# A gated-attention and MLP kernel on one core: the second step's angles copied into the carry tile, five full products for a pair's phases, and a new order table

## The chip, the core and the metric

The kernel runs on one core of a Trainium2 chip. The metric is the device time of one execution in microseconds (us), the median of several runs. One execution was also taken with the hardware profiler; its instructions are shown here by engine: PE (matmul), PEld (the loads of the matmul's weights), DVE, ACT, POOL, and SP, which issues most of the DMAs. PE, DVE, ACT, POOL and SP each run their own instructions strictly in the order in which the program has them, and wait for each other by semaphores.

## The reference

Inputs are q, k, v and a complex gate a (a_re, a_im), each 4 batches x 8 heads x 768 steps x 48. Per batch and head a complex state is multiplied by the gate at each step, k times v is added, and q reads the real part:

```python
mag = np.sqrt(a_re * a_re + a_im * a_im)
scale = np.minimum(mag, 0.999) / (mag + 1e-06)
for t in range(S):
    new_re = ar * S_re - ai * S_im          # ar, ai: the scaled gate at t
    new_im = ar * S_im + ai * S_re
    S_re, S_im = (new_re + kv, new_im)      # kv = outer(k[t], v[t])
    y[:, :, t] = einsum('bhd,bhde->bhe', q[:, :, t], S_re)
```

The heads are then put side by side to x (4 x 768 x 384), and out = x + relu(layernorm(x) * g_ln @ w_ch1) @ w_ch2, with a hidden width of 1536.

## The kernel before

**Tiling.** The steps are cut into chunks of 128; two chunks make a pair. There are 3 pairs per batch and 12 in all, P = 0 to 11; chunk n = 2P + c. Pair 0 is made in two halves of the heads, the others in one piece. The recurrence becomes matmuls: with the running sums of the log magnitudes and of the angles of the gate, k and q are scaled by exp and turned by sine and cosine, and a masked product of the two gives the chunk's part; a state G is carried from chunk to chunk.

**Stages of a pair**, by the names in the order table: `are`, `aim`, `k`, `q`, `vf` are loads. `ln`, `iv`, `r`, `r2`, `u`, `l`, `lc` make the log magnitudes; `dec` sums them on PE, and `e` and `en` are their exponentials. `th` is the angle by arctangent (ACT). `ph` sums the angles on PE into phases; `sin`, `abs`, `cos` (for pairs 0 to 2 a PE step `qt` in place of `abs`) turn them into sine and cosine. `ke`, `qe` scale k and q, `ks`, `qs` multiply by cosine (suffix .0) and sine (.1). `ksT`, `qsT` are the transposes of those, for some chunks on PE (`kT`, `qT`, then a copy), for others by a DMA that SP issues (L617). `am` is the product of chunk n (L635), `atm` its mask on DVE, `gm` and `G` the state, `y` and `x` the chunk's output, `bn` and `rstd` the layer norm, `xtr` and `xT` the transpose of x, `mm1` (L740) and `relu` the first layer, `mm2` (L772), `oa`, `ot`, `st` the second and the store. `wl`, `wp`, `wc` load and prepare the weights once. `warm` is a filler: a product on constants whose result nobody reads.

**Phases.** A pair's tile of angles `th` has on partition p the two steps 2p and 2p+1 (j = 0 and 1). The phase of step t in chunk c is a sum over all earlier steps, so chunk 0 needs partitions 0 to 63 alone, and chunk 1 needs all 128. The sum over the pairs before comes from the tile `car`, of which `pick` selects a row; `car` holds values on partitions 96 to 127 that the pair before has written, and a constant elsewhere. For a pair after the first this makes six products of 384 columns (L498 to L507): three on half of the partitions (64 rows), then three on 128 (or, in a batch's first pair, 96 for the last):

```python
(0, u_th[lo, 0, 0], th[0][lo], True, False),
(1, (pick_f if first else pick)[hi], car[hi], True, False),
(0, u_th[lo, 0, 1], th[1][lo], False, False),
(1, u_th[:, 1, 0], th[0], False, False),
(1, u_th[:, 1, 1], th[1], False, True),
(0, pick[rows], car[rows], False, True)):
```

**Order.** The table `PLAN` names every step once with its engine (P, A, V, G for POOL, S for SP) and, for PSUM users, a bank. The program is emitted in the table's order, so the table sets the order on each engine's queue, and which engine does a step. `@x` behind a step makes it wait for step x as well. Tiles come from small rings (two `car`, two `th`, three `ks`, and so on). Fillers stand in the table where its maker left room on PE.

Of the kernel before, what the change touches and what calls it, by code (L numbers as in the profile page):

```python
# [49 lines left out]
warm.54:P0 warm.55:P0 warm.56:P0 warm.57:P0 dec.1.0:P2 ident:G pad.ks.1:G@pickf en.1.0:A2 q.1.0:S r.2.0:V warm.58:P0  # L50
warm.59:P0 warm.60:P0 warm.61:P0 warm.62:P0 warm.63:P0 warm.64:P0 warm.65:P0 warm.66:P0 warm.67:P0 warm.68:P0
warm.69:P0 warm.70:P0 warm.71:P0 warm.72:P0 warm.73:P0 warm.74:P0 warm.75:P0 dps.0:P5 mask:G are.3.0:S r2.2.0:V
e.1.0:A2 dps.1:P7 ke.0.1.0:V u.2.0:A tab.trig.1:A pad.qs.1:G th.0.1:A vf.0.1:S ke.0.0.0:V th.0.0:A th.1.0:A warm.76:P0
warm.77:P0 warm.78:P0 warm.79:P0 warm.80:P0 warm.81:P0 warm.82:P0 warm.83:P0 warm.84:P0 warm.85:P0 warm.86:P0
# [5 lines left out]
q.2.0:S warm.102:P0 warm.103:P0 warm.104:P0 warm.105:P0 warm.106:P0 warm.107:P0 wp.0:P1 en.2.0:A4 ks.0.0.1:V  # L60
qe.1.0.0:G@qs.0.0.0 car.1.0:V6 wc.0.0:V1 kT.0:P2 e.2.0:A4 wc.0.2:V1 qT.0:P3 vf.1.0:S qt.1.0:P6 vf.1.1:S qsT.0:V3
qT.1:P5 ln.3.0:A qs.1.0.1:G warm.108:P0 warm.109:P0 warm.110:P0 warm.111:P0 kT.1:P3 are.4.0:S ksT.0:A2 q.2.1:S
wc.0.1:V1 qsT.1:V5 iv.3.0:A wl.2:G ksT.1:V3 warm.112:P1 am.0:P0 k.2.1:S aim.4.0:S k.2.0:S warm.113:P2 ph.2.0:P4
am.1:P2 tab.trig.3:A atm.0:V0 atm.1:V2 cos.1.0:A6 v.0:G ke.1.0.1:G warm.114:P0 warm.115:P0 gm.0:P7 y.0:P1 sin.2.0:A4
warm.116:P0 warm.117:P0 qt.2.0:P4 G.0:A7 x.0:A1 qs.1.0.0:V gm.1:P7 y.1:P2 cos.2.0:A4 r.3.0:G xtr.0:P6 x.1:A2
ks.1.0.0:V warm.118:P0 qT.3:P1 pad.qs.2:G qT.2:P4 v.1:G th.3.0:A ks.1.0.1:V xT.0:V6 r2.3.0:G@xT.0 xtr.1:P3 kT.3:P0
qsT.3:V1 wp.2:P6 wl.3:G@xT.0 ksT.3:V0 q.3.1:S qsT.2:A4 tab.log.4:A kT.2:P2 qe.2.0.1:G qe.2.0.0:G am.3:P4 xT.1:V3
G.1:V7 mm1.0.0.1:P0 mm1.0.0.0:P0 one:G@ke.0.1.0 ksT.2:A2 gm.2:P7 relu.0.0:A0 wc.2.0:V6 atm.3:V4 wc.2.2:V6 G.2:A7
mm1.0.1.1:P2 ln.4.0:A am.2:P4 mm1.0.1.0:P2 wc.2.1:V6 y.3:P6 relu.0.1:A2 ph.3.0:P0 iv.4.0:A atm.2:V4 x.3:V6 gm.3:P7
y.2:P6 qs.2.0.1:V x.2:A6 xtr.3:P2 mm1.0.2.1:P4 wl.4:G@atm.2 xtr.2:P3 car.3.0:V0 q.3.0:S r.4.0:G are.6.0:S mm1.0.2.0:P4  # L70
bn.1:V xT.3:V2 xT.2:V3 abs.3.0:A0 mm1.1.1.0:P2 u.3.0:A bn.3:V G.3:V7 relu.0.2:V4 mm1.1.1.1:P2 tab.trig.5:A relu.1.1:A2
mm1.1.2.1:P6 sin.3.0:A0 k.3.0:S bn.2:V mm1.1.2.0:P6 k.3.1:S mm1.1.0.0:P3 cos.3.0:A qs.2.0.0:V are.5.0:S mm1.1.0.1:P3
wl.5:G@qs.2.0.1 l.3.0:V th.4.0:A r2.4.0:V lc.3.0:V qT.5:P2 qT.4:P1 ke.2.0.1:G relu.1.2:V6 mm2.0.0:P5 mm2.0.1:P5
relu.1.0:A3 ke.2.0.0:G ks.2.0.0:G@r2.4.0 tab.log.6:A mm2.1.0:P3 u.4.0:A bn.0:V dec.3.0:P6 rstd.0:A mm2.1.1:P3 qsT.4:V1
e.3.0:A6 mm2.1.2:P3 vf.2.1:S vf.2.0:S qsT.5:V2 l.4.0:V k.4.0:S lc.4.0:V en.3.0:A6 qe.3.0.0:V aim.5.0:S qe.3.0.1:V
vf.3.1:S vf.3.0:S mm2.0.2:P5 ks.2.0.1:G kT.5:P0 dec.4.0:P6 ot.0:V5 oa.1:A3 aim.6.0:S are.7.0:S mm2.2.0:P3 rstd.1:A
dps.3:P5 ksT.5:A0 qs.3.0.0:V qs.3.0.1:V kT.4:P1 decc.3:V5 mm2.2.1:P3 qT.6:P0 ke.3.0.0:V ksT.4:V1 e.4.0:A6 ln.6.0:A
dps.4:P4 qT.7:P2 k.4.1:S mm2.3.0:P1 mm2.2.2:P3 ke.3.0.1:G@ke.3.0.0 ks.3.0.1:V en.4.0:A6 ks.3.0.0:V decc.4:V4 iv.6.0:A
qsT.7:V2 q.4.1:S ln.5.0:A ot.2:V3 v.2:G@ot.2 am.4:P4 ph.4.0:P6 ke.4.0.0:G atm.4:V4 kT.6:P2 qsT.6:A0 gm.4:P0
ot.1:G@atm.4 am.5:P3 ksT.6:V2 mm2.3.1:P1 q.4.0:S kT.7:P5 G.4:V0 iv.5.0:A atm.5:V3 car.4.0:A6 mm2.3.2:P1 r.5.0:G  # L80
tab.trig.7:A abs.4.0:A6 y.4:P2 vf.4.1:S v.3:G sin.4.0:A6 x.4:A2 th.5.0:A ksT.7:V5 st.0:S vf.4.0:S r.6.0:G st.1:S
ot.3:V1 y.5:P0 am.6:P6 x.5:V0 xtr.4:P4 are.8.0:S am.7:P2 xtr.5:P1 q.5.1:S gm.6:P0 xT.4:V4 r2.5.0:G atm.6:V6 cos.4.0:A
ph.5.0:P4 atm.7:V2 xT.5:A1 qe.4.0.1:G@xT.4 G.6:A0 mm1.2.1.0:P6 y.6:P1 q.5.0:S x.6:V1 mm1.2.1.1:P6 mm1.2.2.1:P2
sin.5.0:A4 relu.2.1:V6 abs.5.0:A4 gm.7:P0 G.7:V0 y.7:P4 mm1.2.2.0:P2 aim.7.0:S r2.6.0:A x.7:V4 bn.5:V ke.4.0.1:G
th.6.0:A cos.5.0:A mm1.2.0.0:P0 xtr.7:P5 xT.7:V5 qe.4.0.0:G@atm.6 xtr.6:P4 mm1.2.0.1:P0 xT.6:V4 relu.2.2:A2
tab.log.8:A k.5.0:S qs.4.0.1:V u.5.0:A relu.2.0:V0 k.5.1:S qs.4.0.0:V ks.4.0.0:V mm1.3.1.0:P2 mm1.3.1.1:P2
mm1.3.0.1:P4 l.5.0:V mm1.3.0.0:P4 relu.3.1:A2 ks.4.0.1:V mm2.4.0:P1 ksT.8:S lc.5.0:V u.6.0:A relu.3.0:A4 l.6.0:V
ln.7.0:A mm2.4.1:P1 mm2.5.0:P6 qsT.9:S vf.5.1:S aim.8.0:S v.4:G dec.5.0:P4 mm1.3.2.0:P2 kT.9:P7 iv.7.0:A lc.6.0:V
mm2.5.1:P6 gm.8:P0 e.5.0:A4 ln.8.0:A bn.4:V en.5.0:A4 mm1.3.2.1:P2 bn.7:V mm2.4.2:P1 G.8:V0 bn.6:V relu.3.2:A2 st.2:S
dec.6.0:P4 ksT.9:V7 r.7.0:G qT.8:P2 qsT.8:V2 rstd.2:A k.7.1:S mm2.6.0:P7 k.6.0:S gm.9:P0 qe.5.0.1:G@G.8 en.6.0:A4  # L90
ke.5.0.0:G iv.8.0:A e.6.0:A4 mm2.6.1:P7 r2.7.0:A am.8:P2 k.6.1:S qe.5.0.0:G mm2.5.2:P6 are.9.0:S q.7.0:S G.9:V0
ke.5.0.1:G@qsT.8 ot.4:V1 rstd.3:A q.6.1:S u.7.0:A am.9:P4 vf.5.0:S atm.8:V2 tab.trig.9:A atm.9:V4 ot.5:V6 ph.6.0:P0
th.7.0:A car.6.0:V0 y.8:P2 mm2.6.2:P7 mm2.7.0:P4 y.9:P3 sin.6.0:A0 x.9:A3 mm2.7.1:P4 x.8:V2 qs.5.0.0:G r.8.0:G
abs.6.0:A0 ks.5.0.0:V xtr.8:P5 mm2.7.2:P4 qs.5.0.1:V xT.8:V5 th.8.0:A oa.7:A4 st.3:S ke.6.0.0:G@qs.5.0.1 qT.11:P3
ot.6:V7 xtr.9:P2 bn.9:V xT.9:V2 cos.6.0:A ph.7.0:P0 car.7.0:A0 dps.6:P2 st.4:S abs.7.0:A0 r2.8.0:A ks.5.0.1:V
mm1.4.1.1:P4 mm1.4.1.0:P4 mm1.4.0.1:P6 bn.8:V ke.6.0.1:G qsT.11:V3 kT.11:P3 ksT.10:S q.6.0:S ks.6.0.1:V sin.7.0:A0
relu.4.1:A4 mm1.4.0.0:P6 mm1.4.2.1:P0 mm1.4.2.0:P0 l.7.0:V ksT.11:V3 relu.4.0:A6 tab.log.10:A v.5:V lc.7.0:V
dec.7.0:P4 decc.6:V2 qT.10:P3 ks.6.0.0:V qe.6.0.1:G@ks.6.0.0 aim.9.0:S e.7.0:A4 ln.9.0:A vf.6.0:S gm.10:P6 en.7.0:A4
# [113 lines left out]
def kernel(  # L212
# [123 lines left out]
    def c_pickf():  # L336
        nc.vector.memset(pick_f, 0.0)
        nc.vector.memset(pick_f[ds(HALF, 1)], 1.0)
# [503 lines left out]
```

## Time and profile before

| | |
|---|---|
| three runs | 189.17, 189.30, 191.72 us; median 189.3 |
| the profiled execution's own time | 188.27 us |
| its span (first to last instruction) | 186.6 us, so 1.67 us lie around it |
| PE busy | 176.6 us (95%), 2040 matmuls |
| DVE, ACT, POOL busy | 158.3 (85%), 156.2 (84%), 96.3 (52%) |
| granted clock of PE | 1.0 in every slice |
| moved by DMA | 37.23 MB |

A matmul's own length in the trace is a latency: matmuls overlap, and the next starts before the last has ended. What a matmul costs PE is the time from its start to the next one's start. In the chain of waits a piece is the time until the next piece begins, so pieces there can be added.

### The profile page before, as it was taken

Reading aid. Unit: us, or ns where it says so; the run is one execution under the profiler, and the core shown is the slowest. Engines: PE = TensorE matmul, PEld = TensorE weight load, DVE = VectorE, ACT = ScalarE, POOL = GpSimd, SP = SyncE. Lnnn points to the kernel's source line nnn. Section 1 sums busy time; section 2 is a strip of 40 time slices with the busy share of each in tenths; the row PEclk is TensorE's granted clock in tenths of the full one; section 3 lists DMA queues with packets and bytes.
Section 4 is the critical chain, followed back from the end, with each engine's and each line's share of the span. In section 5 each row is a group of like instructions: output and inputs, shape, how many; then the busy total and the mean of one; then the engine's idle time right before and its main releaser. Section 6 shows DMA issues by size and latency. Waiting matters only on the chain.

```text
span 186.6 us, 5141 instructions
## 1 busy us (share of the span) xinstructions
PE 176.6 (95%) x2040; PEld 136.9 (73%) x2040; DVE 158.3 (85%) x292; ACT 156.2 (84%) x223; POOL 96.3 (52%) x117
## 2 busy tenths in 40 slices
PE   5899999999999999999999999999999899798992
PEld 4678677888676897767877787878868577685772
DVE  0699999999989999889999899988999777576463
ACT  5789999999999999999999999989999878243220
POOL 8137387686614990596058660750613408521650
PEclk9999999999999999999999999999999999999999
DMA  5999999899899998999999999999989999996423
GB/s 141 291 227 186 244 224 220 174 204 233 149 216 251 209 275 185 201 223 210 179 233 228 164 203 282 184 231 181 204 186 195 193 196 182 233 117 168 142 93 127
DMA packets 131799, 37.23 MB, mean 200 GB/s; under 512 B 125888, under 2 KB 131776, under 8 KB 131776
## 3 DMA queue, kind: packets, MB, share of 16 engines
q1 hardware_dynamic: 128272, 33.76, 87.5%
q0 software_dynamic: 2784, 2.36, 8.6%
q10 hardware_dynamic: 720, 0.79, 1.2%
q8 instruction: 16, 0.26, 0.6%
q14 instruction: 7, 0.06, 0.1%
HBM read 28.31 MB, written 4.72 MB: 177 GB/s over the span
## 4 chain that ended last, share of the span: by engine, by line
PE 71%; DMA 13%; DVE 8%; SPq 3%; ACT 2%; issue 1%; POOL 0%; DVEq 0%
PE banks L772 23%; PE banks L740 20%; PE banks L612 5%; PE banks L506 5%; PE banks L635 5%; DMA qsT<-qs 5%; DMA w1b<-in_moe_w_ch_dram 4%; PE banks L481 3%; DMA aim<-in_a_im_dram 3%; PE banks L685 3%; DMA ksT<-ks 2%; DVE w1b L392 2%; PE banks L688 2%; PE banks L706 2%; PE banks L663 2%; SPq L449 1%
## 5 line engine op out<-in xcount | busy, mean ns | idle before, releaser
L772 PE MATMUL banks<-w2b,h 128*128 128x384 bf16 (+1 forms) x300 | 54.6, 319 | 0.0
L740 PE MATMUL banks<-xT,w1b 128*128 128x256 bf16 x432 | 51.3, 272 | 0.1
L740 PEld LDWEIGHTS <-w1b 128*128 128x128 bf16 x432 | 41.2, 98 | 6.4 <-DVE xT L290 0.8
L772 PEld LDWEIGHTS <-h 128*128 128x128 bf16 x300 | 26.8, 97 | 12.4
L293 DVE TENSOR_TENSOR atm<-banks,mask 128x1024 bf16<-128x1024 f32 x24 | 28.9, 1219 | 5.0 <-PE banks L635 4.8
L757 ACT ACTIVATE h<-banks 128x1024 bf16<-128x1024 f32 (+1 forms) x25 | 24.9, 1006 | 8.8 <-PE banks L740 8.5
L293 POOL TENSOR_TENSOR ke<-k,en 128x384 bf16<-128x384 f32 x17 | 16.7, 990 | 16.7 <-ACT en L485 4.6
L810 ACT ACT_TABLE_LOAD x18 | 23.1, 1283 | 1.1 <-PEq L826 0.8
L805 PE MATMUL banks<-u_e 128*128 128x256 f16 x119 | 17.5, 299 | 2.5 <-POOL u_e L322 2.2
L759 DVE TENSOR_SCALAR h<-banks 128x1024 bf16<-128x1024 f32 (+1 forms) x12 | 14.0, 1176 | 4.2 <-PE banks L740 4.1
L635 PE MATMUL banks<-qsT,ksT 128*128 128x128 bf16 x192 | 14.6, 219 | 2.7 <-DMA qsT<-qs 1.7
L293 POOL TENSOR_TENSOR qe<-q,e 128x384 bf16<-128x384 f32 x13 | 11.9, 920 | 10.1 <-DVE ks L293 5.4
L805 PEld LDWEIGHTS <-u_e 128*128 128x128 f16 x119 | 12.5, 107 | 4.9 <-POOL u_e L322 1.9
L635 PEld LDWEIGHTS <-ksT 128*128 128x128 bf16 x192 | 12.2, 97 | 4.8 <-issue 2.3
L785 POOL TENSOR_TENSOR ot<-ot,x 128x384 f32<-128x384 f32 x11 | 11.0, 1003 | 6.2 <-DVE x L290 4.3
L293 POOL TENSOR_TENSOR r<-aim,are 128x768 f16<-128x768 f32 x6 | 10.9, 1815 | 6.0 <-ACT are L454 6.0
L288 ACT CAST x<-banks 128x384 bf16<-128x384 f32 x16 | 7.7, 484 | 7.1 <-PE banks L688 6.2
L698 DVE BATCH_NORM_STATS2 stats<-x 128x6 f32<-128x384 bf16 x24 | 13.2, 550 | 0.3 <-ACT x L288 0.3
L293 POOL TENSOR_TENSOR qs<-qe,trig 128x768 bf16<-128x768 bf16 x6 | 10.4, 1727 | 6.0 <-DVE qe L293 2.9
L418 POOL TENSOR_SCALAR v<-vf 128x768 bf16<-128x768 f32 x8 | 6.7, 839 | 12.8 <-DMA vf<-in_v_dram 10.1
L470 DVE SCALAR_TENSOR_TENSOR l<-r,w 128x768 f16<-128x768 f16 (+1 forms) x13 | 12.4, 954 | 0.7 <-ACT r L466 0.6
L685 PE MATMUL banks<-v,atm 128*128 128x48 bf16 x192 | 11.9, 183 | 0.0
(100 smaller groups left out, 385.9 us busy)
## 6 DMA issues: line engine op xcount, KB each, us to landing
k<-in_k_dram SPq DMA_DIRECT2D x24, 192.0 KB, 4.3
q<-in_q_dram SPq DMA_DIRECT2D x24, 192.0 KB, 4.5
vf<-in_v_dram SPq DMA_DIRECT2D x24, 192.0 KB, 4.1
are<-in_a_re_dram SPq DMA_DIRECT2D x11, 384.0 KB, 5.3
aim<-in_a_im_dram SPq DMA_DIRECT2D x11, 384.0 KB, 4.4
out_dram<-ot SPq DMA_DIRECT2D x20, 192.0 KB, 3.3
w1b<-in_moe_w_ch_dram POOLq DMA_DIRECT2D x3, 384.0 KB, 6.7
w2b<-in_moe_w_ch_dram POOLq DMA_DIRECT2D x3, 384.0 KB, 7.8
```

What stands on the lines that cost most here:

```text
L293: {"DVE": nc.vector, "POOL": nc.gpsimd}[eng(name)].tensor_tensor(**kw)
L470: nc.vector.scalar_tensor_tensor(out=S_("l"), in0=S_("r2"), scalar=0.5, in1=S_("w"), op0=ALU.mult, op1=ALU.add)
L635: nc.tensor.matmul(ps[:, h], lhsT=T("ksT", n)[:, h], rhs=T("qsT", n)[:, h], start=True, stop=True)
L685: nc.tensor.matmul(ps[:, h], lhsT=T("atm", n)[:, h], rhs=T("v", P)[:, c, h], start=True, stop=nfirst)
L698: nc.vector.bn_stats(out=T("stats", n), in_=T("x", n))
L740: nc.tensor.matmul(ps[:, jj], lhsT=w1b[:, dc, ts(gi * JG + jj, C)], rhs=T("xT", P)[:, dc].rearrange("p c t -> p (c t)"), start=(dc == 0), ...
L757: act(out=dst, in_=src, func=AF.Relu)
L759: nc.vector.tensor_scalar(out=dst, in0=src, scalar1=0.0, scalar2=None, op0=ALU.max)
L772: nc.tensor.matmul(bank(own)[:, 0:w], lhsT=T("h", P)[:, j, ts(c, C)], rhs=w2b[:, j, es], start=(j == 0), stop=(j == NJ - 1))
L785: nc.gpsimd.tensor_tensor(out=T("ot", n)[:, es], in0=T("ot", n)[:, es], in1=T("x", n)[:, es], op=ALU.add)
L805: g.add(f"warm.{i}", lambda i=i: nc.tensor.matmul(bank(f"warm.{i}")[:, 0:256], lhsT=u_e[:, 0, 0], rhs=u_e[:, 1].rearrange("p j t -> p (j t ...
L810: g.add(f"tab.{nm}.{i}", lambda tab=tab: nc.scalar.preload_act_table_set(tab))
```

## The change

Two new constant matrices, `u_car` and `u_car_f`, have the sum matrix of chunk 0's second step in rows 0 to 63 and the rows of `pick` (or `pick_f`) in rows 64 to 127. A new step `tc.P` copies the second step's angles of partitions 0 to 63 into partitions 0 to 63 of `car`, where `pick` has zeros. One full product with `u_car` then does what two products did, and the list for a pair after the first has five products, all on 128 rows.

```diff
+    u_car = pool.tile([C, C], FP16, name="u_car")
+    u_car_f = pool.tile([C, C], FP16, name="u_car_f")
...
+    def c_ucar():
+        for t, p in ((u_car, pick), (u_car_f, pick_f)):
+            nc.vector.tensor_copy(out=t[HALF:C], in_=p[HALF:C])
+            nc.vector.tensor_copy(out=t[0:HALF], in_=u_th[0:HALF, 0, 1])
...
+    g.add("ucar", c_ucar, needs=["uth", "pick", "pickf"])
...
+            if NS == 1:
+                def f_tc(X=X, fs=fs, step=step):
+                    dst, src = heads(T("car", P)[0:HALF, fs]), step(T("th", P), 1)[0:HALF]
+                    if eng(f"tc.{X}") == "POOL":
+                        nc.gpsimd.tensor_scalar(out=dst, in0=src, scalar1=1.0, scalar2=0.0,
+                                                op0=ALU.mult, op1=ALU.add)
+                    else:
+                        put(f"tc.{X}", dst, src)
+                add(f"tc.{X}", f_tc, needs=[f"th.{X}", f"car0.{P % RINGS['car']}"],
+                    uses=[("th", P), ("car", P)])
...
-                    lo, hi, th = slice(0, HALF), slice(HALF, C), [step(T("th", P), j) for j in range(R)]
+                    th = [step(T("th", P), j) for j in range(R)]
...
-                            (0, u_th[lo, 0, 0], th[0][lo], True, False),
-                            (1, (pick_f if first else pick)[hi], car[hi], True, False),
-                            (0, u_th[lo, 0, 1], th[1][lo], False, False),
-                            (1, u_th[:, 1, 0], th[0], False, False),
-                            (1, u_th[:, 1, 1], th[1], False, True),
-                            (0, pick[rows], car[rows], False, True)):
+                            (0, u_th[:, 0, 0], th[0], True, False),
+                            (1, u_th[:, 1, 0], th[0], True, False),
+                            (1, u_th[:, 1, 1], th[1], False, False),
+                            (0, u_car_f if first else u_car, car, False, True),
+                            (1, pick_f if first else pick, car, False, True)):
...
             add(f"ph.{X}", f_ph, needs=[f"th.{X}", "uth", "pick", "pickf", f"car0.{P % RINGS['car']}"]
+                + ([f"tc.{X}", "ucar"] if NS == 1 else [])
```

The table `PLAN` is replaced as a whole. It has 1158 steps where it had 1143: eleven `tc` (8 on POOL, 2 on DVE, that of pair 1 on ACT), `ucar` on DVE, and 122 fillers for 119. Among the other steps some change engine: `G.0` goes from ACT to DVE, `G.10` and `G.12` the other way; `abs.10` and `car.10` go from DVE to ACT; `relu.11.0` and `relu.11.1` go from DVE to ACT; `ks.9.0.0` goes from DVE to POOL. Two tokens of the new table: `tc.5.0:G@ksT.7` and `ks.9.0.0:G@xT.17`. The order moves on every engine; three places are shown.

**PE, the phases of pair 4.** `th_92` holds the angles of pair 4, `car_167` its carry. Before:

```order
L506 LDWEIGHTS u_th
L506 MATMUL banks<-th_92,u_th 128x384
L506 LDWEIGHTS pick
L506 MATMUL banks<-car_167,pick 128x384
L506 LDWEIGHTS u_th
L506 MATMUL banks<-th_92,u_th 128x384
L506 LDWEIGHTS u_th
L506 MATMUL banks<-th_92,u_th 128x384
L506 LDWEIGHTS u_th
L506 MATMUL banks<-th_92,u_th 128x384
L506 LDWEIGHTS pick
L506 MATMUL banks<-car_167,pick 128x384
```

and after:

```order
L526 LDWEIGHTS u_th
L526 MATMUL banks<-th_92,u_th 128x384
L526 LDWEIGHTS u_th
L526 MATMUL banks<-th_92,u_th 128x384
L526 LDWEIGHTS u_th
L526 MATMUL banks<-th_92,u_th 128x384
L526 LDWEIGHTS u_car
L526 MATMUL banks<-car_167,u_car 128x384
L526 LDWEIGHTS pick
L526 MATMUL banks<-car_167,pick 128x384
```

The first three of the six were on 64 rows each; all five of the new ones are on 128, and the carry's two stand last.

**DVE and POOL, where k of pair 9 is turned** (`ks_110` is its tile, written once by cosine and once by sine; `car_168` is the carry that pair 10 leaves). DVE before:

```order
L293 TENSOR_TENSOR ks_110<-ke_107,trig_101 128x16x48
L698 BN_STATS stats_142<-x_138 128x6
L699 BN_AGGR mv_149<-stats_142 128x2
L290 COPY xT_156<-banks 128x3x128
L527 TENSOR_SCALAR car_168<-banks 32x384
L293 TENSOR_TENSOR ks_110<-ke_107,trig_101 128x16x48
L551 TENSOR_REDUCE sh_104<-banks 128x768
```

DVE after:

```order
L295 TENSOR_TENSOR qs_113<-qe_109,trig_101 128x16x48 x2
L295 TENSOR_TENSOR ke_107<-k_73,en_100 128x384
L295 TENSOR_TENSOR ks_110<-ke_107,trig_101 128x16x48
L292 COPY xT_156<-banks 128x3x128
L292 COPY dec_94<-banks 48x8 x2
L809 SCALAR_TENSOR_TENSOR ot_162<-banks,rstd_153,x_137 128x384
```

and POOL after:

```order
L295 TENSOR_TENSOR qe_109<-q_70,e_98 128x384
L806 TENSOR_TENSOR ot_165<-ot_165,x_135 128x384
L295 TENSOR_TENSOR ks_110<-ke_107,trig_101 128x16x48
L428 TENSOR_SCALAR v_79<-vf_77 128x768
L295 TENSOR_TENSOR ke_106<-k_74,en_99 128x384
L506 TENSOR_SCALAR car_168<-th_93 64x384
```

The second of the two multiplications stood on DVE behind the carry of pair 10; it now stands on POOL, and the carry has gone to ACT. The last POOL row is one of the new copies, that of pair 11.

**ACT, the last part of the program** (`h_161` is the hidden layer of pair 11; the DMA rows are stores that ACT issues itself). Before:

```order
L778 ACTIVATE ot_162<-banks,rstd_151 128x384
L795 DMA out_dram<-ot_165 128x384
L795 DMA out_dram<-ot_164 128x384
L757 ACTIVATE h_161<-banks 128x512
L795 DMA out_dram<-ot_166 128x384
L778 ACTIVATE ot_163<-banks,rstd_151 128x384
L795 DMA out_dram<-ot_165 128x192 x2
```

and after:

```order
L799 ACTIVATE ot_162<-banks,rstd_151 128x384
L816 DMA out_dram<-ot_165 128x384
L778 ACTIVATE h_161<-banks 128x1024
L799 ACTIVATE ot_163<-banks,rstd_151 128x384
L816 DMA out_dram<-ot_166 128x384
L816 DMA out_dram<-ot_162 128x384
L778 ACTIVATE h_161<-banks 128x1024
L778 ACTIVATE h_161<-banks 128x512
L816 DMA out_dram<-ot_165 128x192
```

Two of the three thirds of the last hidden layer come to ACT, and two stores stand between them.

More of the change, by code (lines that the diff above doesn't have):

```diff
@@ L50 @@
[L50 to L54, printed above, removed]
@@ L60 @@
[L60 to L64, printed above, removed]
@@ L65 @@
[L65 to L98, printed above, removed]
-u.8.0:A relu.4.2:V0 mm2.9.0:P7 qsT.10:V3 G.10:V6 qe.6.0.0:V vf.6.1:S mm2.9.1:P7 am.11:P2 st.6:S iv.9.0:A rstd.4:G
@@ new lines @@
+ke.9.0.1:V atm.16:V3 mm1.7.2.1:P0 gm.16:P2 q.9.1:S relu.7.0:A6 st.9:S am.17:P5 k.10.1:S q.10.0:S relu.7.2:A0
+mm2.14.0:P7 rstd.7:G atm.17:V5 y.16:P4 qe.9.0.1:G x.16:V4 r.11.0:V G.16:A2 qs.9.0.0:V ot.13:G dec.10.0:P0 y.17:P5
+mm2.15.0:P6 k.9.0:S en.10.0:A0 ph.10.0:P2 mm2.15.1:P6 vf.9.0:S qs.9.0.1:V x.17:A5 e.10.0:A0 r2.11.0:A car.10.0:A2
+ke.9.0.0:V xT.16:S mm2.15.2:P6 xtr.17:P1 vf.9.1:S ks.9.0.1:V xT.17:V1 u.11.0:A tab.trig.15:A dps.9:P5 sin.10.0:A2
+k.10.0:S decc.9:V5 ks.9.0.0:G@xT.17 mm2.14.1:P7 q.10.1:S qsT.18:S ksT.18:S ot.15:V6 v.9:G@ks.9.0.1 mm1.8.1.0:P4
```

156 lines of the change are left out of this document (99 added, 57 removed).

## The prediction, as it was put on record before the changed kernel ran

> **What bounds the kernel now.** I read the page's engine lines first, then the chain of waits, then what PE waits for, then busy time by stretch.
>
> ```profile
> PE 176.6 (95%) x2040; PEld 136.9 (73%) x2040; DVE 158.3 (85%) x292; ACT 156.2 (84%) x223; POOL 96.3 (52%) x117
> PE 71%; DMA 13%; DVE 8%; SPq 3%; ACT 2%; issue 1%; POOL 0%; DVEq 0%
> ```
>
> PE is busy nearly all the time, and 71% of the chain that ended last is PE itself. The next view lists what PE stood idle for.
>
> ```profile
> PE banks L805 <- POOL u_e L322: 2.2, 1, 2.2
> PE banks L635 <- DMA qsT<-qs: 1.7, 3, 0.9
> PE banks L635 <- DMA ksT<-ks: 1.0, 1, 1.0
> ...
> ```
>
> Columns are the total, the number of waits, the longest. The first row is the start, as the few short ones left out are, and fillers cover further waits there. Later only 2.7 us remain, all for `am` (L635) on a transposing DMA; the chain below puts them near the end. In between PE runs without a stop:
>
> ```profile
> 20.00:140.00 120.00, 119.58 (x1449) 92.20 (x1447) 113.20 (x208) 117.47 (x164) 68.28 (x66) 1.00 1.02 211
> ```
>
> After the length come busy PE, PEld, DVE, ACT, POOL, the clock and the DMA share. From 20 to 140 us PE's work is the time; but ACT with 117.47 of 120 and DVE with 113.20 are close behind. After that PE waits for transposes. So a product taken from PE before 140 us should count in full, one taken later only where no transpose ends the wait.
>
> **The change, part by part.**
>
> *Phases on PE.* Counting products, six become five. The chain and PE's own rows around pair 4 show what they cost:
>
> ```profile
> 49.39 0.65 PE banks L481 x4
> ...
> 57.90 1.02 PE banks L506 x6
> ...
> 59.83 0.45 PE banks L635 x8
> 57.30 0.61 PE L635 MATMUL banks<-qsT,ksT 128*128 128x128 bf16 x8
> 57.84 0.33 PE L506 MATMUL banks<-th,u_th 64*128 64x384 f16 x1
> 57.84 0.33 PE L506 MATMUL banks<-car,pick 64*128 64x384 f16 x1
> 58.01 0.75 PE L506 MATMUL banks<-th,u_th 64*128 64x384 f16 x3
> 58.60 0.33 PE L506 MATMUL banks<-car,pick 128*128 128x384 f16 x1
> 58.76 0.61 PE L612 MATMUL banks<-ident,ks 128*128 128x128 bf16 x8
> ```
>
> The four products of 384 columns of L481 take 0.65 us, 0.163 each. The first two half products start in the same instant (57.84): they run side by side, and the pair costs 0.17 to the next start. So in products alone this list costs five slots, 5 x 0.163 = 0.81. But from the eight products of L635 at 57.30, which take 0.45 elsewhere, to L612 at 58.76 are 1.46 us: the phases cost 1.46 - 0.45 = 1.01, as the chain's 1.02 says. The 0.20 beyond five slots lies at two seams: the eight L635 products take 0.54 to the first half product instead of 0.45 (0.09), and the three starts from 58.01 to 58.60 cost 0.59 where two slots and a half-row one would be 0.49 (0.10). Both are places where PE goes from full to half rows or back. Five full products have no such seam: 0.81. That is 0.21 saved per pair, 11 pairs: 2.3 us. Those of pair 11 lie between two transposes that PE waits for, so I count ten: **-2.1**.
>
> The Trainium skill, "TensorEngine Tiling (Array Packing)", Tiling Modes, Key Properties, has two rules on this. Different tiles of the array can load and multiply in parallel; by this alone the merging gains nothing on PE, since the two half products already share a slot (the trace agrees on the slot: both start at 57.84). It also says that a change of the tiling mode drains TensorE; by that each list pays twice, and the trace agrees with about 0.09 to 0.10 each. By the first rule alone my sum would lack the 2.1.
>
> *The new copies.* No row shows them. The nearest:
>
> ```profile
> L355 POOL MEMSET car<- 128x384 f16 x2 | 0.8, 413 | 0.0
> L418 POOL TENSOR_SCALAR v<-vf 128x768 bf16<-128x768 f32 x8 | 6.7, 839 | 12.8 <-DMA vf<-in_v_dram 10.1 <-DVE ot L788 2.6
> L338 DVE MEMSET pick_f<- 1x128 f16 x1 | 0.2, 165 | 0.1
> 62.46 0.48 ACT L288 CAST x<-banks 128x384 bf16<-128x384 f32 x1 [0.18 <-PE banks L688]
> 62.98 0.84 ACT L489 ACTIVATE th<-r 128x768 f16<-128x768 f16 x1
> 64.25 1.02 PE banks L506 x6
> ```
>
> A POOL copy of 384 elements is between the fill of the same width, 0.41, and the copy of twice as many, 0.84; I take 0.45, close to half of the latter and to the former. POOL is 52% busy, so eight times 0.45 hide there. What counts is whether the phases wait: `th`, then the copy, then `ph`. In the tightest place, pair 5, the angles end at 63.82 and the phases of the chain stand at 64.25, 0.43 later; the copy with its hand-over would just not fit. But the new table puts `th.5` ahead of `x.4`, the 0.48 in front of it. In the other pairs the angles and the carry end earlier before `ph`. I take **0**, with bounds 0 and +1.2 (two places late by 0.6). Three more fillers stand where PE waits: 0.
>
> *The start.* `ucar` is four copies of 128 columns on DVE, 0.17 each by the nearest row, 0.7 together; `r2.0.1`, a product of half a pair's width, leaves DVE for ACT in exchange, and two of DVE's early waits take more of it. I take 0.15 for what is left. `tc.1` puts about 0.45 on ACT before pair 0's sines, but `th.2` moves behind them. `G.0` goes to DVE:
>
> ```profile
> 28.68 1.24 DVE atm L293
> L290 DVE CAST G<-banks 128x384 bf16<-128x384 f32 x3 | 1.7, 552 | 0.8 <-PE banks L663 0.8
> 33.76 0.69 DVE L290 COPY ksT<-banks 128x1024 bf16<-128x1024 bf16 x1 [0.30 <-PE banks L612]
> ```
>
> It costs 0.55 behind `atm.1`, in front of the `ks`, `qs` and `xT` for which the first `mm1` waits, where DVE has one gap of 0.30. So 0.25 remain. With 0.15: **+0.4**, bounds 0 and +1.0 (0.55 + 0.45 uncovered).
>
> *The transposes near the end.* This is the chain there:
>
> ```profile
> 138.76 0.56 DVE car L527
> 139.34 0.56 DVE ks L293
> ...
> 142.90 4.76 DMA qsT<-qs
> ...
> 147.79 0.61 PE banks L635 x8
> ...
> 153.56 1.34 SPq L617
> ...
> 154.94 4.57 DMA ksT<-ks
> ...
> 159.56 0.62 PE banks L635 x8
> ...
> 166.36 4.03 DMA qsT<-qs
> L293 POOL TENSOR_TENSOR ks<-ke,trig 128x768 bf16<-128x768 bf16 x4 | 6.5, 1640 | 5.2 <-DVE ke L293 2.4 <-DVE r L293 2.3 <-DVE ks L293 0.5
> ```
>
> `ks.9` no longer waits behind the carry (0.56 + 0.56 on DVE), but on POOL it takes 1.64. SP still issues four transposes in a row at about 1.3, and the last lands 4 to 4.8 after its issue. From `xT` to the last landing I find the new chain some 0.2 shorter. From `am.19` to `am.20` the chain is `am` 0.6, two masks' turn 1.3, `qs` 0.6, `ks.10` on POOL 1.7, two issues 2.6, landing 4.6: 11.4, where 159.56 - 147.79 = 11.77 stand now. For pair 11 `qsT` and `ksT` change turns on SP with `ksT` last, which I find 0.3 later. Together **-0.2**; bounds -2.7 (all of the waits gone) and +1.3 (one more issue in front).
>
> *The end.* Now PE ends without a gap:
>
> ```profile
> 175.35 3.94 PE banks L740 x36
> 179.29 3.94 PE banks L772 x36
> 175.05 1.21 ACTq L795 DMA_DIRECT2D out_dram<-ot x2
> 166.77 1.02 ACT L757 ACTIVATE h<-banks 128x1024 bf16<-128x1024 f32 x1 [2.47 <-PE banks L740]
> 179.91 0.58 ACT L778 ACTIVATE ot<-banks,rstd 128x384 f32<-128x384 f32 x1
> ```
>
> After: counted from the start of the last `mm1`, the first third of `mm1` ends after 1.3 and ACT has `relu.11.0` from 1.35 to 2.4, `oa.21` to 3.0, two stores to 4.2, `relu.11.1` to 5.2. PE has done `mm1`, 4 products of 384 and 4 of 192 columns by 3.94 + 0.65 + 0.33 = 4.9 and then needs `relu.11.1`: **+0.4**, bounds 0 and +1.0 (another 0.6 store).
>
> Sum: -2.1 + 0 + 0.4 - 0.2 + 0.4 = -1.5. The profiled execution took 188.27 (span 186.6 and 1.67 around it), so 186.8 by its measure. The median of the three runs, 189.3, is 1.0 above it: **187.8**.
>
> **Rivals.**
>
> *Another engine is the bound.* ACT has 2.5 us idle from 20 to 140, and DVE 6.8. If PE's 2.1 turn into waits for them, only the other terms stay: +0.6, so 189.9. For it: ACT's 98%. Against: nothing of the 119.58 busy of PE shows such a wait now, and by the table ACT loses about as many steps there as it gains.
>
> *The half products were free.* Two of the six share a slot already, so five products cost five slots as six did; if the 0.20 beyond them comes from something that stays (the strided reads of `th`, the hand-over to `ph`), nothing is saved: also +0.6, 189.9. Against: the four starts at L481's pace, which reads its operand with the same stride. The first of the two rules of the Trainium skill above would give this time.
>
> *The waits for transposes go.* -2.1 + 0.4 - 2.7 + 0.4 = -4.0: 185.3. For it: the table takes the carry out of the way of `ks.9`. Against: four issues in a row remain.
>
> *The phases come late by the copy.* `tc` on POOL starts only behind POOL's step in front of it:
>
> ```profile
> L293 POOL TENSOR_TENSOR ke<-k,en 128x384 bf16<-128x384 f32 x17 | 16.7, 990 | 16.7 <-ACT en L485 4.6 <-DVE ke L293 4.5 <-DMA q<-in_q_dram 2.9
> ```
>
> If each of the eight copies is late by such a step, PE waits 8 x 0.99 = 7.9 us: 189.3 - 1.5 + 7.9 = 195.7, slower. It decides from the point at which POOL's copy ends after PE has reached `ph`; pair 5, with 0.43, is nearest to it.
>
> **How the numbers follow.** The forecast has 0.55, its own range 186.7 to 189.0; the transposes' waits gone 0.13 (185.3); another engine 0.17 and free half products 0.07 (both 189.9); late phases 0.08 (195.7). The range 185.3 to 190.2 leaves out the late phases and the ends of the bounds. What this kernel's measurement can tell from no change is about 2%, 3.8 us: faster than 185.5 takes most of the third rival, 0.10; slower than 193.1 is the last, 0.07; the rest, 0.83, is within.
>
> **What would show it.** In the profile after, the chain's `ph` pieces are x5 at 0.81, and the products in front of them keep their usual pace: 0.45 for eight of L635. If they stay near 1.0, the seam is not the row mode. PE's waits must have no row on the carry or on `tc`. Waits of `am` on DMA between 2 and 3.5 us in total confirm the fourth term; a last stretch of `mm2` longer than 3.94 by about 0.4 the fifth. I am wrong if PE's busy time falls and waits on ACT or DVE appear before 140 us.

## The result, and the profile after

The changed kernel takes 195.06 us (median; 193.48 to 195.39) where the kernel before takes 190.13 beside it: a ratio of 1.027 [1.021, 1.033]. It is **slower by 2.7%**, some 5 us; the prediction was 187.8. The profiled execution took 195.39 (span 193.7), 7.1 more than that of before. The page's engine line and the chain:

```profile
PE 174.9 (90%) x2032; PEld 136.8 (71%) x2032; DVE 159.7 (82%) x292; ACT 158.4 (82%) x225; POOL 106.3 (55%) x130
PE 31%; DVE 19%; DMA 17%; SPq 8%; issue 8%; ACT 8%; POOL 6%; ACTq 0%; DVEq 0%; POOLq 0%
```

PE's busy time fell by 1.7 us, near what the five products promised, but PE holds 31% of the chain instead of 71%. Busy time from 20 to 140 us (columns as in the prediction), and what PE waited for:

```profile
20.00:140.00 120.00, 114.47 (x1404) 90.35 (x1404) 115.42 (x203) 111.92 (x156) 74.59 (x76) 1.00 1.02 204
...
PE banks L761 <- DVE xT L292: 3.5, 3, 1.9
PE banks L656 <- DMA ksT<-ks: 3.0, 2, 1.6
PE banks L491 <- DVE l L483: 2.3, 2, 1.9
...
PE banks L656 <- DMA qsT<-qs: 1.3, 1, 1.3
PE banks L656 <- DVE h L780: 1.2, 1, 1.2
```

PE lost 5 us of its 119.58 between 20 and 140, and the new waits are on DVE: just what the prediction had named as the sign that it is wrong. The phases themselves came as forecast, x5 at 0.82 in the chain (1.02 before); one piece shows 0.99, though in PE's rows the next product starts 0.82 after its first:

```profile
67.10 0.82 PE banks L526 x5
108.35 0.99 PE banks L526 x5
```

The three largest waits between 20 and 140 us, in PE's rows (start, length, last column the idle time ahead and what ended it): `mm1.1.1.0` and `mm1.3.1.0` (the hidden layers of pairs 1 and 3) and `am.10`.

```profile
45.19 1.03 PE L761 MATMUL banks<-xT,w1b 128*128 128x256 bf16 x8 [1.87 <-DVE xT L292]
73.86 1.14 PE L761 MATMUL banks<-xT,w1b 128*128 128x256 bf16 x9 [0.87 <-DVE xT L292]
102.03 0.61 PE L656 MATMUL banks<-qsT,ksT 128*128 128x128 bf16 x8 [1.19 <-DVE h L780]
```

A little ahead of each, DVE has one step of 0.55 us that takes three to five times as long, and POOL is busy beside it (the same view, DVE's row first, then POOL's):

```profile
42.23 2.25 DVE L295 TENSOR_TENSOR qs<-qe,trig 128x768 bf16<-128x768 bf16 x1
42.24 1.82 POOL L295 TENSOR_TENSOR r<-aim,are 128x768 f16<-128x768 f32 x1
...
71.41 1.86 DVE L295 TENSOR_TENSOR r<-r 128x768 f16<-128x768 f16 x1
70.53 1.46 POOL L295 TENSOR_TENSOR r<-r 128x768 f16<-128x768 f16 x1
71.95 0.91 POOL L295 TENSOR_TENSOR qe<-q,e 128x384 bf16<-128x384 f32 x1
...
98.36 2.48 DVE L295 TENSOR_TENSOR ks<-ke,trig 128x768 bf16<-128x768 bf16 x1
98.32 0.51 POOL L506 TENSOR_SCALAR car<-th 64x384 f16<-64x384 f16 x1
98.80 1.63 POOL L295 TENSOR_TENSOR ks<-ke,trig 128x768 bf16<-128x768 bf16 x1
```

In each case DVE's step starts while POOL's runs (the first one within 0.01 us of POOL's start) and ends 0.41 to 0.42 us behind POOL's last row (44.48 against 44.06; 73.27 against 72.86; 100.84 against 100.43). The second POOL row of the last group is `ks.6.0.1`, the one ahead of it a new copy, `tc.8`. Behind 140 us PE waits for three transposes (`am.18`, `am.20`, `am.23`), 4.3 us in all by the view of waits where 2.7 stood before:

```profile
151.56 0.62 PE L656 MATMUL banks<-qsT,ksT 128*128 128x128 bf16 x8 [1.41 <-DMA ksT<-ks]
166.09 0.61 PE L656 MATMUL banks<-qsT,ksT 128*128 128x128 bf16 x8 [1.35 <-DMA qsT<-qs]
178.14 0.62 PE L656 MATMUL banks<-qsT,ksT 128*128 128x128 bf16 x8 [1.62 <-DMA ksT<-ks]
```

So the theory to test (**A**): the time went where POOL holds up DVE, because the new order no longer keeps the two apart; the rivals are that the products bring nothing (**B**), that the copies themselves cost the time (**C**), that the stretched steps only stand beside the loss (**D**). A turn, below, is an `@` that makes a POOL step start behind a named DVE step. All ratios below are to the kernel before, run beside each kernel, with a 95% interval; where two kernels are compared with each other, the difference in us is taken from their ratios.

### The profile page after: what moved, and what is told of

The parts are those of the page before. It is cut to its first block, busy times and chain, and to the rows that moved or that the text cites. A ratio compares the mean times of both kernels' runs of the same rounds, so it can differ in the third digit from the quotient of the medians.

```text
span 193.7 us, 5148 instructions
## 1 busy us (share of the span) xinstructions
PE 174.9 (90%) x2032; PEld 136.8 (71%) x2032; DVE 159.7 (82%) x292; ACT 158.4 (82%) x225; POOL 106.3 (55%) x130
## 3 DMA queue, kind: packets, MB, share of 16 engines
HBM read 28.31 MB, written 4.72 MB: 171 GB/s over the span
## 4 chain that ended last, share of the span: by engine, by line
PE 31%; DVE 19%; DMA 17%; SPq 8%; issue 8%; ACT 8%; POOL 6%; ACTq 0%; DVEq 0%; POOLq 0%
PE banks L761 10%; PE banks L793 7%; DMA k<-in_k_dram 5%; SPq L638 4%; DMA out_dram<-ot 4%; SPq L418 3%; DVE r L295 3%; DMA qsT<-qs 3%; DMA ksT<-ks 2%; PE banks L656 2%; PE banks L633 2%; DMA aim<-in_a_im_dram 2%; DVE ks L295 2%; DMA vf<-in_v_dram 2%; DVE ot L809 2%
## 5 line engine op out<-in xcount | busy, mean ns | idle before, releaser
L778 ACT ACTIVATE h<-banks 128x1024 bf16<-128x1024 f32 (+1 forms) x26 | 25.8, 1005 | 7.7 <-PE banks L761 7.6
L826 PE MATMUL banks<-u_e 128*128 128x256 f16 x122 | 16.9, 288 | 2.2 <-POOL u_e L326 2.2
L295 POOL TENSOR_TENSOR qe<-q,e 128x384 bf16<-128x384 f32 x13 | 12.6, 966 | 8.8 <-DVE ks L295 2.6
L780 DVE TENSOR_SCALAR h<-banks 128x1024 bf16<-128x1024 f32 (+1 forms) x11 | 12.8, 1165 | 4.1 <-PE banks L761 4.1
L806 POOL TENSOR_TENSOR ot<-ot,x 128x384 f32<-128x384 f32 x11 | 10.1, 922 | 9.8 <-ACT ot L799 6.4
L295 POOL TENSOR_TENSOR ks<-ke,trig 128x768 bf16<-128x768 bf16 x6 | 9.9, 1651 | 8.8 <-DVE xT L292 4.7
L495 ACT ACTIVATE en<-banks 128x768 bf16<-128x768 f32 (+1 forms) x13 | 9.9, 760 | 3.1 <-PE banks L491 3.1
L295 DVE TENSOR_TENSOR qs<-qe,trig 128x768 bf16<-128x768 bf16 (+1 forms) x21 | 12.2, 593 | 0.1
```

The source lines that it names most:

```text
L295: {"DVE": nc.vector, "POOL": nc.gpsimd}[eng(name)].tensor_tensor(**kw)
L495: add(f"{nm}.{X}", lambda nm=nm, sc=sc, X=X, fs=fs, view=view: act(out=T(nm, P)[:, 0:R, fs], in_=view(f"dec.{X}"), func=AF.Exp, scale=sc), ...
L778: act(out=dst, in_=src, func=AF.Relu)
L780: nc.vector.tensor_scalar(out=dst, in0=src, scalar1=0.0, scalar2=None, op0=ALU.max)
L806: nc.gpsimd.tensor_tensor(out=T("ot", n)[:, es], in0=T("ot", n)[:, es], in1=T("x", n)[:, es], op=ALU.add)
L826: g.add(f"warm.{i}", lambda i=i: nc.tensor.matmul(bank(f"warm.{i}")[:, 0:256], lhsT=u_e[:, 0, 0], rhs=u_e[:, 1].rearrange("p j t -> p (j t ...
```

## Experiments: what the products are worth

**five_only.** In `f_ph` of before:

```
-  six half and full products
+  (0, u_th[:, 0, 0], th[0]), (1, u_th[:, 1, 0], th[0]), (1, u_th[:, 1, 1], th[1]),
+  (0, pick, car), (1, pick_f if first else pick, car)
```

> The kernel before, its order untouched, with the five full products for the phases of a pair and nothing else: no copies and no second weight table, so the odd angles of partitions 0 to 63 are missing from the phases of a pair's first half. Theory A (the new order makes DVE and POOL stretch each other's steps; the five products are worth what was predicted): 0.21 us less for each of ten pairs, about 2.0 us below the kernel before, 188.1 against 190.1. Theory B (PE's gain turns into waits for another engine, so the products themselves bring nothing): 190.1, no difference.

Measured: 188.07, ratio 0.993 [0.991, 0.996]: 0.8 to 1.8 us less, between the two theories (188.07 is A's number, but the kernel before took 189.22 beside it, not 190.1).

**three_products.** `(1, u_th[:, 1, 1], th[1])` and `(0, pick, car)` left out as well.

> As five_only (order of before, no copies), with two of its five products left out as well, so that parts of the phases are missing: another 0.33 us less work on PE in each of eleven pairs. Theory A (PE's work is the time from 20 to 140 us, so that what is taken from PE counts): 3.3 us below five_only's 188.1, 184.8. Theory B (ACT and DVE are as late as PE, which only waits more): 187.6 to 188.2, no more than 0.5 below five_only.

Measured: 188.59, ratio 0.993 [0.989, 0.996], the same as with five. For these 3.3 us of work B holds. The busy time from 20 to 140 us of five_only, then of three_products, and some of PE's waits in the latter:

```profile
20.00:140.00 120.00, 118.68 (x1442) 93.30 (x1441) 113.10 (x208) 117.47 (x165) 68.97 (x66) 1.00 1.01 211
...
20.00:140.00 120.00, 116.33 (x1421) 90.87 (x1419) 113.70 (x209) 117.21 (x166) 68.58 (x66) 1.00 1.01 207
...
PE banks L632 <- ACT trig L552: 1.0, 1, 1.0
PE banks L536 <- ACT trig L529: 0.6, 1, 0.6
...
PE banks L660 <- POOL v L418: 0.5, 1, 0.5
...
PE banks L588 <- DVE xT L290: 0.4, 1, 0.4
```

PE has less to do, DVE and ACT stay where they were, and PE waits now for each of the others in turn. PE was the last engine only by a little over 1 us. The starts of PE's products show the small waits that busy time hides: counting as late what comes later than the quickest tenth of the same two products in all runs, 20 to 140 us hold 1.6 us of lateness before (0.42 by busy time), 3.3 with five products and 6.7 with three. This is an estimate from the rows.

**five_act_light.** five_only with `iv` of `P` = 1 to 11 on `[:, 0:384]` only.

> As five_only, with iv on ACT done for half of the columns only (the other half of r is not what it should be) in ten pairs: about 0.32 us less on ACT each, 3.2 us in all; nothing else changes. Theory B: 1 to 2 us below five_only, 186 to 187, as PE can now use what the products saved. Theory A (PE is the bound): 188.1 as five_only.

Measured: 188.06, ratio 0.990 [0.987, 0.993]; the intervals overlap. ACT's busy time from 20 to 140 us fell by 3.1 (114.36 for 117.47), so ACT alone is not the next bound either.

## Experiments: the order or the copies

**five_old_order.** The plan of before with the copies in it:

```
+tc.1.0:A tc.2.0:G tc.3.0:G tc.4.0:G@qe.3.0.1 tc.5.0:V tc.6.0:G@qs.4.0.1 tc.7.0:G@qs.5.0.1
+tc.8.0:G@l.7.0 tc.9.0:G tc.10.0:G@qs.9.0.1 tc.11.0:G ucar:G
-ke.6.0.1:G
+ke.6.0.1:G@ks.5.0.1
```

> The whole change of computation in the order of before: eleven copies are put into the old table where the engine stands idle (nine on POOL, one each on ACT and DVE, four of POOL's behind a DVE step that they could collide with), and the weight tables are built on POOL at 17.7 us instead of on DVE at 8.7. Theory A: the gain of the five products stays but for some tenths that the copies cost, 188.1 to 189.0. Theory C (the copies themselves, and not the order, cost the time): 3 us or more above the kernel before, 193 to 195.

Measured: 190.12, ratio 1.004 [1.001, 1.007]: C is out as the main cause, but A's number is missed by 1 us. One reason is a collision that I made myself. The copy `tc.5` on DVE, and `r.6.0` on POOL:

```profile
64.62 1.77 DVE L291 COPY car<-th 64x384 f16<-64x384 f16 x1
64.46 1.82 POOL L294 TENSOR_TENSOR r<-aim,are 128x768 f16<-128x768 f32 x1
```

PE waited 0.94 us at the phases of pair 5 for this copy and 0.65 right behind them: here phases did come late by a copy.

**five_old_turn.** `r.6.0:G` becomes `r.6.0:G@tc.5.0`.

> The whole change in the order of before, as in five_old_order, with one turn more: r.6.0 on POOL behind the copy tc.5 on DVE, which took 1.77 us instead of 0.24 to 0.33 there because it started 0.16 us inside r.6.0. Theory A: the wait of mm1.2.1.0 (1.9 us) goes and the kernel comes to 188.2 to 188.7, as fast as the five products alone or nearly. Theory D: 190, nothing changes.

Measured: 189.20, ratio 0.999 [0.996, 1.002]: 0.5% below five_old_order, as fast as before. One turn paid about 0.9 us, less than the 1.6 of those two waits, and just clear of the noise. What the products gain (0.7%, five_only), the copies and their weight tables take back.

**late_five.** Copies and five products for `P > 3` only.

> The change for pairs 4 to 11 alone, in the order of before with the turn of five_old_turn: pairs 1 to 3 keep six products and have no copies, since their copies pushed sin.0.0 on ACT and v.0, ke.1.0.1 and r.3.0 on POOL later by 0.5 to 0.8 us and the first mm1 by 1.1. If the start then stands as before: 0.5 to 1.0 us below five_old_turn's 189.2, 188.2 to 188.7, which would be 0.5 to 0.8% faster than the kernel before. If other copies cost as much: no difference from five_old_turn.

Measured: 190.10, ratio 1.002 [0.999, 1.005]: the hoped-for gain is not there, and the intervals overlap with five_old_turn's. In its profiled execution the slowest load of `w1b` took 8.4 us to land (6.8 before), and PE waited 1.8 for it; whether that is chance, these runs don't tell.

**six_new_order.** Before's code with after's plan, without its `tc` and `ucar` (`pad.e.1`, which waited for `ucar`, waits for `lc.0.0`).

> The reverse: the six products of before, no copies and no second weight table, in the order of after. Theory A: the lost time belongs to the order. Against 195.1 of after, +2.1 for the products, -1.4 because the copy that collides with ks.6.0.0 is gone, -0.8 for a start without the weight tables: about 195, still 4 to 5 us above the kernel before. Theory C: 190 to 191, as before.

Measured: 192.63, ratio 1.017 [1.012, 1.022]. The new table alone costs 3.1 us of the 5.1; I had expected all of it. Two of PE's waits, for the late `xT` and the late `h`:

```profile
PE banks L740 <- DVE xT L290: 1.7, 1, 1.7
...
PE banks L635 <- DVE h L759: 0.8, 1, 0.8
```

`ks.6.0.0` took 2.01 us here without any copy in front of it (2.48 in after), held by `ks.6.0.1`, which the new table moves from DVE to POOL.

**six_turns.** The same with two turns more:

```
-r.4.0:G  ks.6.0.1:G
+r.4.0:G@qs.2.0.1  ks.6.0.1:G@ks.6.0.0
```

> As six_new_order (the six products of before in the order of after) with two turns: r.4.0 behind qs.2.0.1, ks.6.0.1 behind ks.6.0.0. If the order cost its 3.1 us by collisions: the stalls at mm1.1.1.0 (1.84) and am.10 (1.0) go, 189.6 to 190.6 against 192.6. If it costs them by itself: 192 to 193.

Measured: 189.74, ratio 1.000 [0.997, 1.003]. Neither wait is left: all that the new table cost, within the interval, lay in two collisions.

**turns_no_copies.** six_turns with the five products of five_only.

> As six_turns (the new order, two turns, no copies and no second weight table), with the five full products, so that the odd angles of partitions 0 to 63 are missing from the phases of a pair's first half. If the copies and the tables hold the remaining 2.3 us: 188.5 to 189.7, as or a little below six_turns (189.7), since PE's own saving is partly taken by other waits as in five_only. If it is the five products in this order that bring the waits: 191 to 192.

Measured: 190.41, ratio 1.008 [1.004, 1.011], between the two. Here five products are 0.8% slower than six in the same order. Its PE is mostly ahead of six_turns from 105 to 158 us, by up to 0.5, and waits longer for the transposes of `am.20` (1.49 against 0.56) and `am.23` (1.67 against 0). SP issued the last transpose of each no later (156.37 against 156.58, 168.70 against 169.29), but they took 4.95 and 4.72 us to land against 4.30 and 3.17. Why is open.

## Experiments: turns taken and given

**turns_three.** After, with

```
-r.4.0:G  r2.5.0:G  tc.8.0:G
+r.4.0:G@qs.2.0.1  r2.5.0:G@r2.6.0  tc.8.0:G@ks.6.0.0
```

> After, with three POOL steps told to start behind the DVE step that they stretched: r.4.0 behind qs.2.0.1 (2.25 us instead of 0.55), r2.5.0 behind r2.6.0 (1.86 instead of 0.56), tc.8.0 behind ks.6.0.0 (2.48 instead of 0.55). Order and steps stay. Theory A: PE's stalls at these three places (2.0, 1.0 and 1.4 us) go, up to 4.4 us: 190.7 if all of it comes back, 192 to 193 if other waits take half. Theory D (PE's stalls have other causes, such as the loads and transposes by DMA, and the stretched steps only stand beside them): 194 to 195.

Measured: 192.04, ratio 1.012 [1.006, 1.017], 2.9 us less than after. A holds, D is out. PE's waits between 35 and 140 us in its profiled execution, of which the first is new:

```profile
PE banks L684 <- DVE G L292: 0.4, 1, 0.4
...
PE banks L761 <- DVE xT L292: 0.2, 1, 0.2
```

The waits for `xT` (2.7 of after's 3.5 lie in this stretch) are 0.2 and the 1.2 of `am.10` is gone: 3.7 us of stalls went and 2.9 of time. In the profiled execution part of it was taken back at the start, where the first `mm1` came at 38.03 us (36.26 in after), and by the small new waits; the waits for transposes at the end stayed (4.0 against 4.3).

**one_turn_more.** Only the first of the three.

> After with a single turn more: r.4.0 on POOL behind qs.2.0.1 on DVE, which took 2.25 us instead of 0.55. Theory A: mm1.1.1.0 comes 1.6 to 1.8 us earlier, and as PE is late there for nothing else the kernel gains 1.2 to 1.8: 193.2 to 193.9 against 195.1. Theory D: no difference.

Measured: 193.31, ratio 1.019 [1.015, 1.023], 1.6 us less than after. DVE's step has its usual length, and POOL's stands behind it (the profile names ACT for POOL's idle time, but in after the same step started at 42.24 without that):

```profile
42.06 0.56 DVE L295 TENSOR_TENSOR qs<-qe,trig 128x768 bf16<-128x768 bf16 x1
42.76 1.80 POOL L295 TENSOR_TENSOR r<-aim,are 128x768 f16<-128x768 f32 x1 [0.72 <-ACT r L476]
```

**one_turn_less.** Before, with `ks.2.0.0:G@r2.4.0` as `ks.2.0.0:G`.

> The kernel before with a single turn taken out: ks.2.0.0 on POOL may start when its operands are there (about 45.0 us) and not behind r2.4.0 (47.13). Theory A: qs.2.0.0 and l.3.0 on DVE start inside POOL's two steps of 1.64 and take about 1.8 and 2.4 us instead of 0.52 and 0.95; DVE is some 2.7 late, and the kernel 1.0 to 2.5 us slower than before. Theory D: POOL is done 2 us earlier and nothing gets slower.

Measured: 192.40, ratio 1.012 [1.007, 1.016], 2.2 us slower though POOL's two steps run 2 us earlier. DVE's two steps, POOL's pair, and the two waits of PE that are new:

```profile
45.37 1.82 DVE L293 TENSOR_TENSOR qs<-qe,trig 128x768 bf16<-128x768 bf16 x1
47.11 2.39 DVE L470 SCALAR_TENSOR_TENSOR l<-r,w 128x768 f16<-128x768 f16 x1
45.13 3.55 POOL L293 TENSOR_TENSOR ks<-ke,trig 128x768 bf16<-128x768 bf16 x2
...
PE banks L481 <- DVE h L759: 1.2, 1, 1.2
...
PE banks L612 <- DVE qs L293: 0.6, 1, 0.6
```

**before_no_turns.** All 29 `@` of before taken out.

> The kernel before with its 29 turns (a POOL step told to start behind a named DVE step) taken out; the order of steps on each engine stays. Theory A (a DVE step with two operands in SBUF that starts inside a POOL step is held until POOL pauses): POOL's steps start earlier, DVE's rows show several steps of 0.55 us at 1 to 2.5, and the kernel is 1 to 5 us slower, 190.5 to 194. Theory D (the stretched steps are no cause of lost time): POOL's earlier steps do no harm, 188.5 to 190.

Measured: 203.97, ratio 1.077 [1.071, 1.083]. Far more than expected: about 14.5 us, of which PE has 9.95 at the first `mm1` (45.05 against 35.10). Behind 20 us 20 of DVE's steps are held by over 0.15 us (4 before). Since the loads `wl` lose their turns too, and the granted clock fell to 0.7 to 0.8 in two of the 40 slices, not all of it need be DVE's.

## Experiments: the start and the end

**turns_start.** turns_three with `ucar:V` taken out and `ucar:G@qe.0.1.0` behind `wl.0`, both ahead of `pad.ks.2` on POOL (`pad.e.1` waits for `r.1.0` instead).

> After with the three turns of turns_three, and the second weight tables built on POOL at about 19 us instead of on DVE at 8.7 us, where the four copies took 1.1 us of the chain of decays. If the 1.1 us lie on the path to the first mm1: 0.7 to 1.0 us below turns_three, 191.1 to 191.3 against 192.0. If the start is set by the loads alone: no difference.

Measured: 191.40, ratio 1.012 [1.007, 1.016]; no difference from turns_three.

**turns_ks9.** turns_three with `ks.9.0.0:V` behind `ks.9.0.1:V`.

> After with the three turns of turns_three, and ks.9.0.0 (0.55 us on DVE, 1.64 on POOL) back on DVE behind ks.9.0.1, as it stood before. If the wait of am.18 (1.6 us, for a transpose of ks.9) comes from POOL's slower step and its turn: 1.0 to 1.5 us less, 190.6 to 191.0. If SP's row of transposes sets the landing anyway: at most 0.3 less.

Measured: 191.73, ratio 1.012 [1.008, 1.017]; no difference, and `am.18` waits 1.45 (1.46 in turns_three). So POOL's slower step doesn't set it. SP's row alone doesn't either: its transpose took 5.38 us from issue to landing here, and 3.42 in turns_all2 below, which has the same row there and no wait of `am.18`. What sets that time is open.

**turns_tail.** turns_ks9 with SP's row changed:

```
-k.10.0:S q.10.1:S qsT.18:S ksT.18:S qsT.19:S ksT.19:S   qsT.22:S qsT.23:S ksT.23:S
+qsT.18:S ksT.18:S qsT.19:S ksT.19:S k.10.0:S q.10.1:S   ksT.23:S qsT.22:S qsT.23:S
```

> As turns_ks9 (after, three turns, ks.9.0.0 on DVE), with SP's row changed in two places: the loads k.10.0 and q.10.1 behind the four transposes of pair 9 instead of ahead of them (1.46 us of issues), and ksT.23 ahead of qsT.22, into the 1.75 us in which SP waits for qs.11.0.0. If SP's row sets the landings: the waits of am.18 (1.6 us) and am.23 (1.8) nearly go, 2 to 3 us below turns_ks9's 191.7, 189 to 189.7. If DMA's own time sets them, or am.20 takes the wait instead: at most 0.8 less.

Measured: 194.36, ratio 1.022 [1.018, 1.026], a miss of 5 us by the medians. The waits of `am.18` and `am.23` did go, and a larger one came:

```profile
149.10 0.75 DVE L295 TENSOR_TENSOR qe<-q,e 128x384 bf16<-128x384 f32 x1 [5.10 <-DMA q<-in_q_dram]
151.51 0.66 PE L491 MATMUL banks<-l,u_e 128*128 128x384 f16 x3 [3.65 <-DVE l L483]
```

DVE stood 5.1 us at `qe.10` for the load that I moved, and behind it in DVE's row stood `l.11` and `lc.11`, for which PE waits. I had counted the time that `qe.10` may be late, not what stands behind it.

**turns_all.** turns_tail, turns_start and four turns more (two of them in place of an earlier `@`).

> All together: turns_tail, the weight tables on POOL as in turns_start, and four turns more where DVE's rows still show a held step (ke.5.0.0 behind qe.5.0.0, qe.4.0.1 behind ks.4.0.0, ke.10.0.0 behind l.11.0, qe.9.0.0 behind l.10.0). If the causes found are all there is: 188.2 to 189.5, no slower than before. If POOL, now late by these turns, holds up others: 190 to 191.

Measured: 193.38, ratio 1.019 [1.015, 1.023], with the same wait (DVE 5.69 us, PE 4.77).

**turns_all2.** turns_all with the two loads put back.

> As turns_all, with k.10.0 and q.10.1 again ahead of the transposes of pair 9; ksT.23 stays ahead of qsT.22. If the moved loads made the wait ahead of dec.11.0 and the exchange of the transposes is a gain: am.18 waits 1.5 us again, dec.11.0 no more, am.23 not at all: 3 us below turns_all's 193.4, 189.6 to 190.6. If the four further turns hold POOL up: 191 to 192.5.

Measured: 188.68, ratio 0.997 [0.994, 1.000], 4.1 us below turns_all and 5.7 below after: the change is brought back to where the kernel before stands, though it is not clearly faster. That is about 1 us below what I had expected: the wait of `am.18` did not come back (`am.19` waits 0.45). The transposes of pair 11 in SP's row, of turns_ks9 and then of turns_all2, and two rows of PE of the latter (`am.22` and `am.23`, without a wait):

```profile
164.01 1.29 SPq L638 DMA_TRANSPOSE ksT<-ks  x1
167.06 2.61 SPq L638 DMA_TRANSPOSE qsT<-qs  x2
169.73 1.34 SPq L638 DMA_TRANSPOSE ksT<-ks  x1
...
161.40 2.68 SPq L639 DMA_TRANSPOSE ksT<-ks  x2
164.66 2.62 SPq L639 DMA_TRANSPOSE qsT<-qs  x2
...
168.16 0.61 PE L657 MATMUL banks<-qsT,ksT 128*128 128x128 bf16 x8
170.27 0.61 PE L657 MATMUL banks<-qsT,ksT 128*128 128x128 bf16 x8
```

SP stood 1.76 us for `qs.11` with `ksT.23` behind it; issued into that gap, it leaves PE no wait at `am.23` (1.63 in turns_ks9).

## Why the prediction was wrong, point by point

The forecast was -1.5 us, the measurement +5.1. The step that failed is the sum: it had no term for which POOL step now runs beside which DVE step, and that cost 3.1 us. "POOL is 52% busy, so eight times 0.45 hide there" counts the time that POOL has, not whom its steps hold up. The other 2.0 us came with the five products and their copies. That is not the copies alone: without any copy, five products in the new order cost 1.5 us more than six (turns_no_copies against six_turns), and the cause of that is open.

*What bounds the kernel.* This reading failed first: "PE's work is the time" from 119.58 busy of 120. A matmul's length in the rows (0.33 us) is twice what it costs (0.163) and so covers small waits, and ACT (117.47) stood as close as I had noted. three_products shows what the view could not: with an estimated 5.4 us less work, the kernel saves no more than with 2.1.

*Phases on PE, -2.1.* The mechanism was right: 0.82 for five without a seam, by the row. The size was not, for the reason above: -1.3 in the old order (five_only). "Another engine is the bound" was the rival that said so.

*The copies, 0.* The question was put wrongly. In after no wait of PE on a copy appeared; the rival of late phases came near the time (195.7) by luck, through a thing that did not happen there. A copy's cost is also whom it holds: `tc.8`, 0.51 long, stood ahead of `ks.6.0.0` and, with the POOL step behind it, made 0.55 into 2.48; without the copy it was 2.01 (six_new_order).

*The order.* It cost most: 3.1 us (six_new_order), all of it in two collisions (six_turns). I had read the new table for what is removed and added on each engine's row, never for which DVE and POOL steps come to stand beside each other; the turns were in the plan to see, and `r.4.0` has none. Nor is it order alone. The two tables differ in the engine of 53 steps, not only of those named ahead of the prediction (where `G.12` goes from ACT to DVE, not the other way): 25 move between DVE and POOL. `ks.6.0.1` (DVE to POOL) made one of the two collisions, and `r2.6.0` (ACT to DVE) stands in the one at 71.41.

*The start, +0.4.* The first `mm1` came 1.16 later in the trace; but with the tables off DVE (turns_start) the median did not move and the first `mm1` still came at 36.05 (35.10 before), so its cause is not shown.

*The transposes, -0.2.* +1.6 by PE's waits (4.3 against 2.7). "`ksT` last, which I find 0.3 later" was 2.0: from the issue of `qsT.22` to the last landing were 5.36 us before and 7.35 after, and the waits of `am.22` and `am.23` together went from 0.86 to 1.62. I counted SP's issues, but not that SP first waits for `qs.11`, so that `ksT.23` pays behind that wait.

*The end, +0.4.* 0: from the first `mm1` of pair 11 to PE's end are 8.02 us in both.

The Trainium skill has the rule that was missing, in "SBUF — State Buffer", section "Who interferes with whom": VectorE's second pair of SBUF ports is GpSimd's only one, an exclusive lock; a VectorE instruction with two SBUF inputs contends with a GpSimd one that reads SBUF, and one in a two-port mode (copies and `tensor_scalar` can be) contends as well, while one with a single SBUF input outside these modes does not. The counts in the last section agree. The page also says that the second to start waits until the first has ended; the rows differ in one point, that at 71.41 and 98.36 DVE waited through two POOL steps.

What stays open: why five products are slower than six in the new order with its turns, what sets the 3 to 5 us until a transpose lands, and how much of the rest each of turns_all2's edits holds.

## What to carry to other kernels

Where DVE and POOL both read SBUF, an order is judged by pairs: for every DVE step with two SBUF operands on the path, ask which POOL step may run when it starts, and give that one a turn behind it. A hundredth of a microsecond can decide: `qs.2.0.1` of after, 0.01 ahead of POOL's `r.4.0` in the trace, was still held for 1.70 us. An engine busy for 99.6% of a stretch need not be its only bound if another has 98%: take away more of its work and see whether the time follows. And a transfer moved back in a queue costs what stands behind its reader, not the reader's slack.
